# Block-causal attention and a three-way maxout FFN on one core: the limits of the weights' upper words on GpSimd, the weights' transfers begun by SyncE, other durations in the planner

## The chip, the cores and the metric

The kernel runs on one core of a Trainium2 chip. The metric is the device time in microseconds. The core has five engines, each with its own queue worked through in order: TensorE (PE; its weight loads are shown as PEld), VectorE (DVE), ScalarE (ACT), GpSimd (POOL) and SyncE (SP), which here only begins transfers. An instruction waits at the head of its queue until the semaphores that it needs are there, and all that stands behind it waits too.

## What is computed

```python
# q, k, v: (8 batches, 8 heads, 576, 64)
scores = scale * np.matmul(q, k.transpose(0, 1, 3, 2))
mask = block_i >= block_j                      # blocks of 64 rows
scores = np.where(mask, scores, -1000000000.0)
attn = np.exp(scores - max) / (sum + 1e-09)
x = (attn @ v).transpose(0, 2, 1, 3).reshape(4608, 512)
h = np.maximum(np.maximum(x @ w1, x @ w2), x @ w3)   # w1, w2, w3: 512 x 768
out = h @ w_out                                       # 768 x 512
```

The FFN's four weight matrices come as float64; the kernel reads each number as two 32-bit words.

## The kernel before

**Attention.** Heads are worked on in pairs, four pairs per batch. A pair loads q, k (`nat`) and v (`vn`), turns q and k (`kq`), multiplies them (`qk`, and `qk4` for the last 64 rows), takes the row limits (`top`, VectorE, L422), the exponential (ScalarE, L606, L960), the sum and its reciprocal (VectorE), scales (`scale`, on GpSimd or ScalarE, whichever the planner finds free), turns the probabilities and multiplies with v (`pv`, L1000). Batch 0 is done in two halves, front and back pairs, and turns on TensorE (`raise_qk`, `raise_p`, `raise4`) with copies by VectorE or ScalarE (`place...`, L251 or L249). From batch 1 on VectorE turns (`turn_qk` L917, `turn` L629), and SyncE moves the turned blocks (`move`, L641, `pt<-pz`).

**FFN.** A chunk is one half of a batch's rows (256 or 320 columns). For each of six blocks f of the hidden width it has three products with four parts each (`product`, L1118), each product as three matmuls, since x and the weights are each split into a high and a low part; then maximum (`most`, L1133), split (`high`, `low`), and the projection (`project`, L1184).

**Weight units.** The weights are prepared once, in 24 units: unit u = 0 to 17 makes the split blocks of w1, w2 and w3, unit 18 to 23 those of w_out. A unit loads 512 KB (`load`, L292, a transfer begun by GpSimd), then works on 128x512 blocks: `size` on ScalarE (L302, the absolute value of the upper words), five steps on VectorE, namely `clamp` (L308, the limits), `shift` (L315), `sign` (L321), `power` (L327) and `rest` (L338), then `high` on ScalarE, `whole` on TensorE (L345 to L347) and `lower` on ScalarE. The buffers of `a` and `b` are called wo or osb in the profile. No product with a block can start before its unit is done. All 24 units fall in the first 150 us.

**The order.** All work is cut into jobs with a cost per engine, a rank and the jobs they come after. `in_order` is a planner: it plays the jobs through with these costs (`LAG` for the way from one engine to another, `dve()`, `act()`, `pool()` and the constants at the top for durations) and writes down which engine begins which job next; where a job has two engines it takes the first that is free. The program then has exactly this order on each queue. So a changed constant changes the order, and the choice between GpSimd and ScalarE, or ScalarE and VectorE, without any change in the work.

Of the kernel before, what the change touches and what calls it, by code (L numbers as in the profile page):

```python
# [11 lines left out]
I32 = mybir.dt.int32  # L12
# [13 lines left out]

TO_PE = 250.0
LAG = {
    "PE": {"PE": 0.0, "ACT": 200.0, "DVE": 200.0, "POOL": 200.0, "SP": 200.0},
    "ACT": {"PE": TO_PE, "ACT": 0.0, "DVE": 90.0, "POOL": 160.0, "SP": 150.0},  # L30
    "DVE": {"PE": TO_PE, "ACT": 130.0, "DVE": 0.0, "POOL": 155.0, "SP": 150.0},
    "POOL": {"PE": TO_PE, "ACT": 130.0, "DVE": 130.0, "POOL": 0.0, "SP": 150.0},
    "SP": {"PE": 100.0, "ACT": 100.0, "DVE": 100.0, "POOL": 100.0, "SP": 0.0},
}
SEND = 620.0
LOAD = 540.0
ASK = 1000.0
# [3 lines left out]

GAP = 60.0
SMALL = 130.0

RAISE = 215.0
DEBUG = False
# [95 lines left out]
def dve(n, fast=False):  # L142
    return 100.0 + n / (1.92 if fast else 0.96)


def act(n, psum=True):
    return (105.0 if psum else 135.0) + n / 1.2


def pool(n):  # L150
    return 120.0 + 2.6 * n


@with_exitstack
def kernel(
# [11 lines left out]
    nc = tc.nc  # L167
# [17 lines left out]
    TURN = 12  # L185
# [71 lines left out]
    class Unit:  # L257


        def __init__(self, u, src, dst, n, prior, *early, first=None):  # L260
            self.src, self.dst, self.n, self.u = src, dst, n, u
            self.last = n == DO
            rank = DELAY + PACE * u


            self.tag = f"wo{dst}" if self.last else f"w{u}"
            self.temps = (f"wo{u % NF}",) if not self.last else (f"wo{4 + dst % 2}",) if dst < 4 else ("osb", "osb")
            j = self.issued = job(
                {"POOL": ASK},
                rank - 8,  # L270
                self.load,
                after=(prior and prior.issued, first, *(e.sized for e in early if e)),
                take=(self.tag,) if self.last else (),
            )
            j = job({}, 0, lambda eng: None, after=(j,), lasts=MOVE, moved=1600.0)
            j = self.sized = job({"ACT": act(512, False)}, rank, self.size, after=(j,), take=self.temps)
            for step, fast in (
                (self.clamp, True),
                (self.shift, True),
                (self.sign, False),  # L280
                (self.power, True),
                (self.rest, False),
            ):
                c = dve(512, fast)
                j = job({"DVE": c}, rank, step, after=(j,), take=("left",) if step == self.rest else (), lasts=c + GAP)
            j = job({"ACT": act(512, False)}, rank, self.high, after=(j,))
            j = job({"PE": 6 * pe(512)}, rank, self.whole, after=(j,), take=("pm",), give=(*self.temps, "left"))
            self.done = job({"ACT": act(512)}, rank, self.lower, after=(j,), give=("pm",))
# [144 lines left out]
    def norm_cost(n):  # L433
        return {"POOL": 160.0 + 1.86 * n, "ACT": 235.0 + n / 1.2}

# [6 lines left out]
    class Head:  # L442
# [7 lines left out]
        def plan(self, t0):  # L450

            pair, part, self.exps, self.inv = self.pair, self.pair.part, {}, {}
            for n, ts in enumerate(part.groups):
                apart, r = None, t0 + (SECOND if part.beside and ts == part.later else n)
                for t in ts:
                    m = P * (t + 1)
                    d = job(
                        {"DVE": dve(m) + 120.0},
                        r + 1,
# [6 lines left out]
                    if t != ts[-1]:  # L466
                        apart = job({}, 0, lambda eng: None, after=(d,), lasts=GAP)
                    self.exps[t] = job({"ACT": act(m) + 240.0}, r + 2, self.exp, t, after=(d,), take=(f"p{t}",))
                join([self.exps[t] for t in ts], BANK)
# [175 lines left out]
    class Pair:  # L645
# [106 lines left out]
        def plan4(self, first, tq, last):  # L752
            asked = job({"ACT": 2 * act(64, False)}, first - TURN + 2, self.ask, after=(tq,), take=("q8",))
            tops = []
            for a in range(2):
                last = job({"PE": 4 * pe(64 if a else 512)}, first + 3 + a, self.qk4, a, after=(asked, last), take=BANK)
                tops.append(
                    job(
                        {"DVE": dve(64 if a else 512) + 120.0},
                        first + 4 + a,  # L760
# [264 lines left out]
    left = {}  # L1025
# [197 lines left out]
    rank = 0  # L1223
# [54 lines left out]
```

## Time and profile before

| | before |
|---|---|
| median of 3 runs | 927.47 us (925.59 to 927.82) |
| profiled execution | 927.53 us |
| its span, first to last instruction | 925.7 us |
| TensorE busy | 895.4 us, 97% |
| VectorE busy | 530.1 us, 57% |
| ScalarE busy | 479.6 us, 52% |
| GpSimd busy | 246.3 us, 27% |
| mean granted TensorE clock | 0.994 |

The profile is of one execution. A share is an average over the span, so it is read beside the windows: the first 150 us, with the weight units and batch 0, look different from the rest. A busy time is the union of an engine's instructions; a wait of an instruction that has already started, for another engine's hold on something, is inside its duration and not in the idle time. Chain: the work that ended last, followed back to what released it.

### The profile page before, as it was taken

The page shows a single profiled execution, that of the slowest core. Times are in us where ns is not written, and L with a number is a line of the kernel's source. Part 1 is how long each engine was busy: PE and PEld are TensorE (multiplying, and loading weights), DVE is VectorE, ACT ScalarE, POOL GpSimd, SP SyncE. Part 2 cuts the span into 40 slices and gives each one's busy share as a digit, 9 for nine tenths or more (in the row PEclk, how much of TensorE's full clock was granted, in tenths as well). Part 3 has the DMA queues.
Part 4 walks back from the last instruction along what each step waited for, and adds up shares of the span by engine and source line. Part 5 has one row for each costly group of instructions (what it writes and reads, how often), then busy time and mean ns, then how long its engine had stood idle before and what let it go on. Part 6 is the DMA issues. An engine that isn't in the chain of part 4 may idle for free.

```text
span 925.7 us, 16909 instructions
## 1 busy us (share of the span) xinstructions
PE 895.4 (97%) x5880; PEld 744.7 (80%) x5880; DVE 530.1 (57%) x1555; ACT 479.6 (52%) x1359; POOL 246.3 (27%) x377
## 2 busy tenths in 40 slices
PE   6798899999999999999999999999999999999998
PEld 4456667886988888888888888888888888899997
DVE  4999688786674655465574655465664655431101
ACT  3777557655564555556464555555464654522111
POOL 3522232333231222223132222223131322222101
PEclk9999999999999999999999999999999999999999
DMA  6841535576644554555533555555543543330010
GB/s 197 232 144 54 125 85 126 127 141 145 131 94 100 113 123 105 133 110 124 118 86 80 114 123 107 123 111 132 110 99 75 115 113 84 95 73 24 1 35 23
DMA packets 226132, 98.36 MB, mean 106 GB/s; under 512 B 189696, under 2 KB 218368, under 8 KB 226048
## 3 DMA queue, kind: packets, MB, share of 16 engines
q1 hardware_dynamic: 208192, 82.35, 40.3%
q0 software_dynamic: 3456, 12.58, 4.0%
q10 hardware_dynamic: 14400, 2.36, 1.4%
q8 instruction: 46, 0.75, 0.3%
q14 instruction: 38, 0.31, 0.1%
HBM read 41.94 MB, written 9.44 MB: 56 GB/s over the span
## 4 chain that ended last, share of the span: by engine, by line
PE 90%; DVE 5%; ACT 1%; issue 1%; DMA 1%; POOL 1%; ACTq 0%; SPq 0%; DVEq 0%; POOLq 0%
PE pm L1118 49%; PE pm L1184 16%; PE sb L1000 10%; PE sb L933 9%; PE sb L940 3%; PE pm L345 1%; DVE sb L422 1%; DVE wo L321 1%; DVE wo L308 1%; DVE left L338 1%; POOL p L440 1%; DMA nat<-in_q_dram 1%; PE sb L558 0%; ACT w L249 0%; DVE wo L315 0%
## 5 line engine op out<-in xcount | busy, mean ns | idle before, releaser
L1118 PE MATMUL pm<-xh,w 128*128 128x320 f32 (+1 forms) x2304 | 500.2, 304 | 0.7 <-ACT w L249 0.7
L1118 PEld LDWEIGHTS pm<-xh,w 128*128 128x128 f32 x2304 | 379.9, 190 | 20.1 <-issue 15.3
L1118 PE MATMUL pm<-xl,w 128*128 128x256 f32 (+1 forms) x1152 | 341.2, 296 | 0.7 <-POOL xl L254 0.5
L1118 PEld LDWEIGHTS pm<-xl,w 128*128 128x128 f32 x1152 | 219.0, 190 | 7.2 <-issue 5.3
L422 DVE CUSTOM_DVE_ANT_0 sb<-sb,mask 128x512 f32<-128x512 f32 (+3 forms) x288 | 144.8, 529 | 138.3 <-PE sb L940 70.0
L1133 DVE TENSOR_TENSOR m<-pm,m 128x256 f32<-128x256 f32 (+1 forms) x192 | 87.3, 455 | 167.1 <-PE pm L1118 159.0
L606 ACT ACTIVATE p<-sb,nm 128x128 f32<-128x128 f32 (+3 forms) x256 | 134.2, 528 | 75.0 <-DVE nm L422 62.8
L254 POOL TENSOR_TENSOR hl<-m,hh 128x256 fp32r<-128x256 f32 x96 | 71.6, 746 | 316.9 <-ACT hh L249 285.1
L629 DVE STREAM_TRANSPOSE pz<-p 128x512 f32<-128x512 f32 (+1 forms) x280 | 136.4, 525 | 21.8 <-ACT p L438 20.0
L440 POOL TENSOR_TENSOR p<-p,rs 128x384 f32<-128x384 f32 (+4 forms) x129 | 90.0, 719 | 186.7 <-DVE rs L750 180.8
L1184 PE MATMUL pm<-wo,hh 128*128 128x512 f32 x384 | 119.2, 391 | 0.0
L249 ACT CAST hh<-m 128x256 fp32r<-128x256 f32 x96 | 39.0, 406 | 121.3 <-DVE m L1133 120.7
L438 ACT ACTIVATE p<-p,rs 128x512 f32<-128x512 f32 (+4 forms) x159 | 89.6, 608 | 20.2 <-DVE rs L750 12.9
L1000 PE MATMUL sb<-pt,vn 128*64 128x320 f32 (+4 forms) x840 | 90.4, 362 | 4.0 <-ACT p L606 2.5
L254 POOL TENSOR_TENSOR xl<-x,xh 128x256 fp32r<-128x256 f32 (+1 forms) x64 | 51.9, 815 | 156.1 <-ACT xh L249 150.0
L933 PE MATMUL sb<-kq 64*128 64x256 f32 (+3 forms) x512 | 88.5, 466 | 2.6 <-DVE kq L251 2.0
L1000 PEld LDWEIGHTS sb<-pt,vn 128*64 128x64 f32 x840 | 55.3, 137 | 37.4 <-issue 5.0
L1184 PEld LDWEIGHTS pm<-wo,hh 128*128 128x128 f32 x384 | 71.0, 188 | 15.1 <-issue 0.3
L933 PEld LDWEIGHTS sb<-kq 64*128 64x128 f32 x512 | 45.5, 192 | 38.1 <-issue 21.7
L1184 PE MATMUL pm<-wo,hl 128*128 128x512 f32 x192 | 74.8, 390 | 0.0
L249 ACT COPY m<-pm 128x256 f32<-128x256 f32 (+1 forms) x96 | 38.3, 399 | 45.9 <-PE pm L1118 33.3
L249 ACT COPY osb<-pm 128x512 f32<-128x512 f32 x36 | 21.1, 587 | 75.7 <-PE pm L1184 75.7
(82 smaller groups left out, 762.5 us busy)
## 6 DMA issues: line engine op xcount, KB each, us to landing
pt<-pz SPq DMA_DIRECT2D x224, 200.0 KB, 3.9
w<-in_moe_w_dram POOLq DMA_DIRECT2D x18, 512.0 KB, 5.6
vn<-in_v_dram SPq DMA_DIRECT2D x64, 128.0 KB, 2.4
out_dram<-osb SPq DMA_DIRECT2D x32, 256.0 KB, 2.1
nat<-in_k_dram SPq DMA_DIRECT2D x112, 72.0 KB, 2.3
nat<-in_q_dram SPq DMA_DIRECT2D x96, 72.0 KB, 2.7
wo<-in_moe_w_out_dram POOLq DMA_DIRECT2D x6, 512.0 KB, 4.2
nat<-in_q_dram ACTq DMA_DIRECT2D x16, 72.0 KB, 3.2
```

What stands on the lines that cost most here:

```text
L249: nc.scalar.copy(dst, src)
L254: {"DVE": nc.vector, "POOL": nc.gpsimd}[eng].tensor_tensor(out=dst, in0=a, in1=b, op=ALU.subtract)
L422: nc.vector.tensor_tensor_reduce(out=ps, in0=ps, in1=hidden, scale=-SCALE, scalar=first, op0=ALU.add, op1=ALU.min, accum_out=out_)
L438: nc.scalar.mul(p, p, r)
L440: nc.gpsimd.tensor_tensor(out=p, in0=p, in1=r.broadcast_to([P, p.shape[1]]), op=ALU.mult)
L606: nc.scalar.activation(dst, src, AF.Exp, bias=nm[:, c : c + 1], scale=-1.0, accum_out=sm[:, c : c + 1])
L629: nc.vector.transpose(dst, p[:, 0 : n * P])
L933: nc.tensor.matmul(ps, self.q[h.own, P * t : P * (t + 1)], self.k[h.own, 0:w], start=True, stop=True)
L1000: nc.tensor.matmul(o[h.own].rearrange("p (i u) -> p i u", u=n)[:, :, c0 : c0 + z - a], self.vn[:, kt, h.j, :], h.pt[:, :, h.off + a : h.of ...
L1118: nc.tensor.matmul(self.ps, w[i, f][:, c, :], xx, start=(c == 0 and s == 0), stop=(c == NC - 1 and s == 2))
L1133: nc.vector.tensor_tensor(out=m, in0=ps, in1=m, op=ALU.max)
L1184: nc.tensor.matmul(self.po[: self.rows], h, w[f], start=(f == 0 and s == 0), stop=(f == NF - 1 and s == 2))
```

## The change

Three things change. `clamp` is issued to GpSimd instead of VectorE. The 24 transfers of weights are begun by SyncE instead of GpSimd, between its other loads. And the planner's constants are others, so the order on all five queues is another. What is computed, its shapes and its buffers stay the same. Line numbers behind L280 are three higher after the change.

```diff
-TO_PE = 250.0
+TO_PE = 180.0
 LAG = {
     "PE": {"PE": 0.0, "ACT": 200.0, "DVE": 200.0, "POOL": 200.0, "SP": 200.0},
-    "ACT": {"PE": TO_PE, "ACT": 0.0, "DVE": 90.0, "POOL": 160.0, "SP": 150.0},
-    "DVE": {"PE": TO_PE, "ACT": 130.0, "DVE": 0.0, "POOL": 155.0, "SP": 150.0},
...
+    "ACT": {"PE": TO_PE, "ACT": 0.0, "DVE": 140.0, "POOL": 180.0, "SP": 150.0},
+    "DVE": {"PE": TO_PE, "ACT": 120.0, "DVE": 0.0, "POOL": 240.0, "SP": 150.0},
...
 def dve(n, fast=False):
-    return 100.0 + n / (1.92 if fast else 0.96)
+    return 68.0 + n / (1.92 if fast else 0.96)
...
@@ class Unit
             j = self.issued = job(
-                {"POOL": ASK},
+                {"SP": LOAD},
                 rank - 8,
                 self.load,
...
-                c = dve(512, fast)
-                j = job({"DVE": c}, rank, step, after=(j,), take=("left",) if step == self.rest else (), lasts=c + GAP)
+                c = dve(512, fast) + (130.0 if fast else 80.0)
+                e = "DVE"
+                if step == self.clamp:
+                    e, c = "POOL", pool(512)
+                j = job({e: c}, rank, step, after=(j,), take=("left",) if step == self.rest else (), lasts=c + GAP)
...
         def load(self, eng):
...
-            nc.gpsimd.dma_start(st.rearrange("p (c f) -> p c f", f=2 * self.n), self.src.bitcast(I32))
+            nc.sync.dma_start(st.rearrange("p (c f) -> p c f", f=2 * self.n), self.src.bitcast(I32))
...
         def clamp(self, eng):
-            nc.vector.tensor_scalar(
+            nc.gpsimd.tensor_scalar(
                 out=self.a, in0=self.a, scalar1=LOW, scalar2=TOP, op0=ALU.max, op1=ALU.min
             )
...
     def norm_cost(n):
-        return {"POOL": 160.0 + 1.86 * n, "ACT": 235.0 + n / 1.2}
+        return {"POOL": 250.0 + 1.5 * n, "ACT": 190.0 + n / 1.2}
```

The other constants (`GAP`, `SMALL`, `RAISE`, `act()`, `pool()`, the sums added to `top`, `exp` and `ask`) change in the same way. Three places show what this does to the queues. A name such as wo_842 is one buffer of a unit.

First, VectorE's queue where units 12 to 14 are prepared, before the change (L308 is `clamp`, L315 `shift`, L321 `sign`, L327 `power`, L338 `rest`):

```order
L308 TENSOR_SCALAR wo_842<-wo_842 128x512
L327 TENSOR_SCALAR wo_781<-wo_781 128x512
L315 TENSOR_SCALAR wo_842<-wo_842 128x512
L321 SCALAR_TENSOR_TENSOR wo_842<-w_684,wo_842 128x512
L327 TENSOR_SCALAR wo_842<-wo_842 128x512
L308 TENSOR_SCALAR wo_881<-wo_881 128x512
L338 SCALAR_TENSOR_TENSOR left<-w_432,wo_700 128x512
L315 TENSOR_SCALAR wo_881<-wo_881 128x512
```

and after it, about the same units (L318 is `shift`, L324 `sign`, L330 `power`, L341 `rest`, L425 `top`):

```order
L318 TENSOR_SCALAR wo_839<-wo_839 128x512
L1136 TENSOR_TENSOR m<-pm,m 128x256
L324 SCALAR_TENSOR_TENSOR wo_839<-w_633,wo_839 128x512
L318 TENSOR_SCALAR wo_868<-wo_868 128x512
L330 TENSOR_SCALAR wo_839<-wo_839 128x512
L425 ISA sb,nm<-sb,mask 128x512
L425 ISA nm 128x1
L341 SCALAR_TENSOR_TENSOR left<-w_612,wo_717 128x512
L324 SCALAR_TENSOR_TENSOR wo_868<-w_664,wo_868 128x512
```

The row of `clamp` is gone, and steps of attention stand between the unit's steps. On GpSimd's queue the units' rows were transfers (L292):

```order
L254 TENSOR_TENSOR xl_619<-x_0_592,xh_601 128x256
L992 COPY p_578<-p_578 128x64
L292 DMA w_684<-in_moe_w_dram 128x4x256
L292 DMA w_706<-in_moe_w_dram 128x4x256
L292 DMA w_722<-in_moe_w_dram 128x4x256
L254 TENSOR_TENSOR xl_787<-x_1_761,xh_773 128x320
```

and are now limits (L311):

```order
L254 TENSOR_TENSOR xl_546<-x_0_537,xh_539 128x256
L311 TENSOR_SCALAR wo_584<-wo_584 128x512
L311 TENSOR_SCALAR wo_592<-wo_592 128x512
L311 TENSOR_SCALAR wo_600<-wo_600 128x512
L311 TENSOR_SCALAR wo_626<-wo_626 128x512
L311 TENSOR_SCALAR wo_659<-wo_659 128x512
L311 TENSOR_SCALAR wo_671<-wo_671 128x512
L254 TENSOR_TENSOR xl_699<-x_1_681,xh_687 128x320
```

Six limits stand in a row there, those of units 5 to 10. Second, VectorE's queue ahead of the first `turn_qk` of batch 1 (the long transpose), before:

```order
L251 COPY kq<-sb 128x2x64
L338 SCALAR_TENSOR_TENSOR left<-w_722,wo_890 128x512
L251 COPY pz<-sb 128x4x4x32
L251 COPY pz<-sb 128x3x4x32
L917 STREAM_TRANSPOSE kq<-nat 128x1152
```

and after:

```order
L251 COPY kq<-sb 128x2x64
L324 SCALAR_TENSOR_TENSOR wo_946<-w_853,wo_946 128x512
L324 SCALAR_TENSOR_TENSOR wo_995<-w_880,wo_995 128x512
L251 COPY pz<-sb 128x4x4x32
L251 COPY pz<-sb 128x3x4x32
...
L341 SCALAR_TENSOR_TENSOR left<-w_727,wo_933 128x512
L251 COPY pz<-sb 128x4x4x32
L251 COPY pz<-sb 128x3x4x32
L251 COPY pz<-sb 128x4x16
L920 STREAM_TRANSPOSE kq<-nat 128x1152
```

Thirteen rows stand between the copy and the transpose instead of three. Third, SyncE's queue, where it loads `nat` (k) and `vn` (v) of the back pairs of batch 0, before:

```order
L902 DMA vn_76<-in_v_dram 128x4x64 x2
L907 DMA vn_76<-in_v_dram 64x2x64
L875 DMA nat<-in_k_dram 128x4x64 x2
L881 DMA nat<-in_k_dram 64x2x64
L902 DMA vn_75<-in_v_dram 128x4x64 x2
L907 DMA vn_75<-in_v_dram 64x2x64
```

and after (L295 is the transfer of a weight unit, here units 9 to 15):

```order
L905 DMA vn_76<-in_v_dram 128x4x64 x2
L910 DMA vn_76<-in_v_dram 64x2x64
L295 DMA w_595<-in_moe_w_dram 128x4x256
L295 DMA w_602<-in_moe_w_dram 128x4x256
L295 DMA w_612<-in_moe_w_dram 128x4x256
L295 DMA w_633<-in_moe_w_dram 128x4x256
L295 DMA w_664<-in_moe_w_dram 128x4x256
L905 DMA vn_75<-in_v_dram 128x4x64 x2
L910 DMA vn_75<-in_v_dram 64x2x64
L295 DMA w_694<-in_moe_w_dram 128x4x256
L295 DMA w_727<-in_moe_w_dram 128x4x256
```

Seven transfers of weights stand between the loads of v, and the load of k is further back.

## Rows read from the trace of the kernel before

**Rows 1.** The page: busy time by engine; VectorE's busy tenths in 40 slices.

```profile
PE 895.4 (97%) x5880; PEld 744.7 (80%) x5880; DVE 530.1 (57%) x1555; ACT 479.6 (52%) x1359; POOL 246.3 (27%) x377
...
DVE  4999688786674655465574655465664655431101
```

**Rows 2.** Windows of 25 us: length, then PE, PEld, DVE, ACT, POOL busy, PEclk, DMA.

```profile
0.00:25.00 25.00, 16.04 (x70) 10.52 (x70) 12.32 (x48) 10.56 (x32) 9.92 (x23) 1.00 0.73 200
25.00:50.00 25.00, 18.47 (x92) 11.02 (x93) 23.44 (x65) 19.63 (x55) 9.93 (x14) 0.93 0.75 225
50.00:75.00 25.00, 23.02 (x130) 15.88 (x126) 24.07 (x59) 19.00 (x48) 10.54 (x13) 0.93 0.43 127
75.00:100.00 25.00, 22.67 (x129) 15.21 (x130) 20.42 (x50) 17.50 (x42) 7.67 (x11) 1.00 0.23 63
100.00:125.00 25.00, 22.24 (x136) 15.72 (x135) 19.43 (x44) 15.12 (x39) 5.14 (x6) 1.00 0.43 94
125.00:150.00 25.00, 22.96 (x136) 16.81 (x135) 19.57 (x55) 15.39 (x42) 9.11 (x14) 0.93 0.33 79
...
250.00:275.00 25.00, 25.00 (x172) 20.81 (x171) 16.71 (x49) 14.28 (x43) 7.78 (x14) 1.00 0.51 104
```

**Rows 3.** The chain that ended last, in order of time: start, us, what.

```profile
73.92 1.30 DVE wo L308
...
137.56 2.21 PE sb L1000 x20
```

**Rows 4.** The same chain, near 212 us.

```profile
212.23 3.69 DMA pt<-pz
```

**Rows 5.** VectorE's instructions by line and form, 13 to 150 us: busy, mean ns, idle before.

```profile
L338 DVE SCALAR_TENSOR_TENSOR left<-w,wo 128x512 fp32r<-128x512 uint32 x18 | 13.4, 744 | 1.7 <-PE pm L347 1.7
L321 DVE SCALAR_TENSOR_TENSOR wo<-w,wo 128x512 int32<-128x512 int32 x18 | 12.6, 698 | 0.1
L308 DVE TENSOR_SCALAR wo<-wo 128x512 f32<-128x512 f32 x22 | 11.7, 542 | 0.8 <-ACT wo L302 0.8
L327 DVE TENSOR_SCALAR wo<-wo 128x512 int32<-128x512 int32 x22 | 11.4, 516 | 0.2
L315 DVE TENSOR_SCALAR wo<-wo 128x512 int32<-128x512 int32 x22 | 11.1, 510 | 0.2
...
L321 DVE SCALAR_TENSOR_TENSOR wo<-wo,wo 128x512 int32<-128x512 int32 x4 | 4.0, 1003 | 0.1
```

**Rows 6.** Timeline, VectorE at 60 and 73 us, GpSimd at 73 us: start, us, instruction.

```profile
60.42 0.42 DVE L308 TENSOR_SCALAR wo<-wo 128x512 f32<-128x512 f32 x1
...
61.34 0.69 DVE L321 SCALAR_TENSOR_TENSOR wo<-w,wo 128x512 int32<-128x512 int32 x1
...
73.84 1.37 DVE L308 TENSOR_SCALAR wo<-wo 128x512 f32<-128x512 f32 x1
...
73.76 1.16 POOL L440 TENSOR_TENSOR p<-p,rs 128x576 f32<-128x576 f32 x1 [1.19 <-DVE rs L977]
```

**Rows 7.** GpSimd's instructions by line and form, 13 to 150 us.

```profile
L254 POOL TENSOR_TENSOR xl<-x,xh 128x320 fp32r<-128x320 f32 x4 | 3.5, 868 | 25.3 <-ACT xh L249 25.3
...
L440 POOL TENSOR_TENSOR p<-p,rs 128x512 f32<-128x512 f32 x3 | 3.3, 1096 | 0.0
```

**Rows 8.** Window 13 to 150 us: all engines as in rows 2; GpSimd's L292 alone.

```profile
13.00:150.00 137.00, 118.96 (x657) 80.65 (x657) 116.40 (x298) 93.10 (x242) 48.22 (x64) 0.96 0.46 126
...
13.00:150.00 137.00, 15.94 (x22) 0.96 0.46 126
```

**Rows 9.** VectorE's plain copies of turned probabilities, one form, 13 to 150 us.

```profile
L251 DVE COPY pz<-sb 128x256 f32<-128x256 f32 x6 | 2.5, 414 | 0.1
```

**Rows 10.** Waits: VectorE's longest from 13 to 150 us, SyncE's longest of the span.

```profile
DVE kq L917 <- DMA nat<-in_k_dram: 3.8, 1, 3.8
...
SPq L902 <- PE sb L1000: 235.2, 32, 24.1
```

**Rows 11.** The page, transfers: count, KB each, median us from issue to landing.

```profile
w<-in_moe_w_dram POOLq DMA_DIRECT2D x18, 512.0 KB, 5.6
```

More of the change, by code (lines that the diff above doesn't have):

```diff
@@ L24 @@
 EPS = 1e-9
-TO_PE = 250.0
+TO_PE = 180.0
 LAG = {
     "PE": {"PE": 0.0, "ACT": 200.0, "DVE": 200.0, "POOL": 200.0, "SP": 200.0},
-    "ACT": {"PE": TO_PE, "ACT": 0.0, "DVE": 90.0, "POOL": 160.0, "SP": 150.0},
-    "DVE": {"PE": TO_PE, "ACT": 130.0, "DVE": 0.0, "POOL": 155.0, "SP": 150.0},
-    "POOL": {"PE": TO_PE, "ACT": 130.0, "DVE": 130.0, "POOL": 0.0, "SP": 150.0},
+    "ACT": {"PE": TO_PE, "ACT": 0.0, "DVE": 140.0, "POOL": 180.0, "SP": 150.0},
+    "DVE": {"PE": TO_PE, "ACT": 120.0, "DVE": 0.0, "POOL": 240.0, "SP": 150.0},
+    "POOL": {"PE": TO_PE, "ACT": 90.0, "DVE": 130.0, "POOL": 0.0, "SP": 150.0},
     "SP": {"PE": 100.0, "ACT": 100.0, "DVE": 100.0, "POOL": 100.0, "SP": 0.0},
@@ L40 @@
 TURNED = 4400.0
-GAP = 60.0
-SMALL = 130.0
-RAISE = 215.0
+GAP = 85.0
+SMALL = 100.0
+RAISE = 110.0
 DEBUG = False
@@ L142, in dve @@
 def dve(n, fast=False):
-    return 100.0 + n / (1.92 if fast else 0.96)
+    return 68.0 + n / (1.92 if fast else 0.96)
 def act(n, psum=True):
-    return (105.0 if psum else 135.0) + n / 1.2
+    return (52.0 if psum else 88.0) + n / 1.2
 def pool(n):
-    return 120.0 + 2.6 * n
+    return 150.0 + 2.15 * n
 @with_exitstack
@@ L275, in __init__ @@
             j = job({}, 0, lambda eng: None, after=(j,), lasts=MOVE, moved=1600.0)
-            j = self.sized = job({"ACT": act(512, False)}, rank, self.size, after=(j,), take=self.temps)
+            j = self.sized = job({"ACT": act(512, False) + 65.0}, rank, self.size, after=(j,), take=self.temps)
             for step, fast in (
@@ L457, in plan @@
                     d = job(
-                        {"DVE": dve(m) + 120.0},
+                        {"DVE": dve(m) + 35.0},
                         r + 1,
@@ L467, in plan @@
                         apart = job({}, 0, lambda eng: None, after=(d,), lasts=GAP)
-                    self.exps[t] = job({"ACT": act(m) + 240.0}, r + 2, self.exp, t, after=(d,), take=(f"p{t}",))
+                    self.exps[t] = job({"ACT": act(m) + 200.0}, r + 2, self.exp, t, after=(d,), take=(f"p{t}",))
                 join([self.exps[t] for t in ts], BANK)
@@ L752, in plan4 @@
         def plan4(self, first, tq, last):
-            asked = job({"ACT": 2 * act(64, False)}, first - TURN + 2, self.ask, after=(tq,), take=("q8",))
+            asked = job({"ACT": 510.0}, first - TURN + 2, self.ask, after=(tq,), take=("q8",))
             tops = []
@@ L758, in plan4 @@
                     job(
-                        {"DVE": dve(64 if a else 512) + 120.0},
+                        {"DVE": dve(64 if a else 512) + 65.0},
                         first + 4 + a,
@@ L766, in plan4 @@
                 )
-            e = job({"ACT": act(512) + act(64) + 480.0}, first + 5, self.exp4, after=tops, take=("p4",), give=2 * BANK)
+            e = job({"ACT": act(512) + act(64) + 350.0}, first + 5, self.exp4, after=tops, take=("p4",), give=2 * BANK)
             inv = job({"DVE": SMALL}, first + 6, self.sum4, after=(e,), lasts=SMALL + GAP)
```

## The prediction, made before the changed kernel was run

> **What bounds the kernel now.** I read the busy shares and the forty slices first, then the windows of 25 us, then the chain of waits, then the costs of single instructions in the stretch that the windows point to. Over the whole span TensorE is busy 97% and VectorE 57% [rows 1], which says that TensorE bounds the kernel. The windows say when that holds. From about 150 us on TensorE has no idle time at all, 25.00 of 25 us as in the window 250 to 275. Before, it is idle for 8.96, 6.53, 1.98, 2.33, 2.76 and 2.04 us in the first six windows, 24.6 us together, and it starts only 70 to 136 matmuls in each, against 172 later [rows 2]. In the same windows VectorE is busy 23.4 and 24.1 and then 19.4 to 20.4 of 25 us. So there are two programs in this trace: up to about 140 us VectorE feeds TensorE too slowly, and after that nothing but the amount of matmul work counts. The chain agrees: at 73.92 us it runs through weight preparation on VectorE, and from 137.56 us it stays on TensorE [rows 3]. One exception follows: near 212 us the chain leaves TensorE once more for a transfer of the turned probabilities [rows 4].
>
> It follows that time can be won only ahead of 140 us, that a microsecond less of VectorE's queue there brings later matmuls forward by about as much, and that the 24.6 us of idle time (of which the first 4.8 us are the first loads) bound the sum.
>
> **The limits leave VectorE.** Each of 24 weight units has five VectorE steps, and the first, `clamp`, goes to GpSimd. In the stretch from 13 to 150 us 22 of these instructions are busy for 11.7 us, 542 ns each [rows 5]; two more, on other buffers, at the undisturbed 0.42 us [rows 6] make it 12.5 us. VectorE is the engine whose queue binds, so all of it counts: **-12.5 us**. On GpSimd the same instruction is not in the trace. Its nearest rows there are the product over 128x512 at 1.10 us and the difference over 128x320 at 0.87 us [rows 7]; I take 1.1, bounds 0.87 and 1.3 (a fifth more). 24 x 1.1 = 26.4 us. GpSimd is busy 48.2 of the 137 us, 15.9 of them beginning the weights' transfers [rows 8]. Those go, so it ends at 48.2 - 15.9 + 26.4 = 58.7 us, and its own queue doesn't bind. A unit's chain gets about 0.7 us longer. In the new order `shift` waits for GpSimd, and VectorE's queue stands behind it; the new order puts copies, tops and steps of other units between, as the order shows, so I price this wait at nothing. Were that cover gone, it would cost up to 24 x 0.7 = 17 us.
>
> **What the two engines do to each other.** An undisturbed step over 512 columns takes 0.42 us; one that started at 73.84 us took 1.37 while GpSimd had a product in hand from 73.76 to 74.92 [rows 6]. So a VectorE step waits until GpSimd's instruction ends. Over the undisturbed 0.42 and 0.69 us, the other four steps lose (0.510 - 0.42) x 22 = 2.0, (0.516 - 0.42) x 22 = 2.1, (0.698 - 0.69) x 18 + (1.003 - 0.69) x 4 = 1.4 and (0.744 - 0.69) x 18 = 1.0 us, 6.5 together [rows 5, 6]. These 96 steps stay, and GpSimd computes more. If only its arithmetic holds VectorE up, that grows from 48.2 - 15.9 = 32.3 to 58.7 us, a factor of 1.8, and 6.5 becomes 11.8 us: +5.3. If beginning transfers holds it up as much, the factor is 58.7 / 48.2 = 1.2, and the cost is +1.4. The long wait that I can see was arithmetic, so I take **+5.3 us**, with 1.4 as the other end.
>
> The Trainium skill, "SBUF — State Buffer", section "Who interferes with whom", says that a VectorE instruction in a two-port mode and a GpSimd instruction exclude each other for the whole of the one that came first, and that writing the descriptors of a GpSimd-issued transfer needs the same ports. The 1.37 us agree with its first half. Its second half would count the transfers' beginnings too, and by it the sum would be 3.9 us better than mine; its first half speaks against putting more work on GpSimd beside VectorE, and that is the first rival below.
>
> **Copies.** In the order VectorE has 51 plain copies where it had 47: 11 more of turned probabilities, seven fewer of others. At 0.41 us [rows 9] four are **+1.6 us**. ScalarE, which gets these seven and loses the eleven, is busy 93.1 of 137 us [rows 8] and doesn't bind.
>
> **The new order.** VectorE's longest wait in the stretch is 3.8 us, for the keys of the first pair of batch 1, ahead of `turn_qk` [rows 10]. The order puts three rows between the copy whose matmuls free the loads' buffer and this transpose now, some 1.9 us of work (0.69, 0.68 and 0.55), and 13 rows after the change, about 6.6 us. That would cover the wait. But in SyncE's queue the loads of two weight units now stand right ahead of that load. I take half: **-1.9 us**, bounds 0 and -3.8. The remaining moves of the order (attention of batch 0 earlier against the weights, matmuls of the first chunk ahead of the units they don't need) put more work ahead of TensorE while weights are made; I count nothing for them. After 220 us TensorE is never idle, its order differs by less than 1.4 us of matmuls at any place that I compared, and the same work remains: 0.
>
> **The transfers go to SyncE.** 24 issues, 15.9 us on GpSimd for 22 of them, land in SyncE's queue. That queue mostly waits: its `vn` loads wait 235 us in all for matmuls that free their buffer [rows 10]. That is also the danger, since SyncE works in order: units 9 to 13 stand behind a `vn` load that needs the values matmul of the last front pair, 14 and 15 behind a later one. From that values matmul to unit 9's own TensorE had 104 matmuls before and has 153 in the new order, some 28 us at the 130 and 136 per 25 us of [rows 2]. A weight block lands 5.6 us after its issue [rows 11], five in a row take up to four issues more, and the seven steps of a unit add up to 4.6 us at the durations above. So it is hidden: 0. If the cover is gone, a unit is late by about the 5.6 us of one transfer, once.
>
> **The stall at 212 us.** It hangs on turns that VectorE does and matmuls that TensorE does in the same stretch; both come forward alike, so it stays: 0. Were it to go, it would be worth up to the 3.7 us of that transfer [rows 4].
>
> **The sum.** -12.5 + 5.3 + 1.6 - 1.9 = -7.5 us. The profiled execution took 927.53 us (span 925.7 and 1.8 around it), the median of the runs is 927.47, so they may be taken as one: 927.5 - 7.5 = **920.0 us**. With the kind ends of the unknowns it is -12.5 + 1.4 + 1.6 - 3.8 - 3.7 = -17, or 910.5; with the unkind ones, ahead of any rival, -12.5 + 6.3 + 1.6 = -4.6 (clamps of 1.3 us, a factor of 63.5 / 32.3), or 923.
>
> **Rivals.** *First, the exclusion eats the gain, and more.* The clamp of one unit ends and GpSimd begins the next instruction just as VectorE is told to go on with `shift`; the new GpSimd order has six clamps in a row. If every clamp holds up one VectorE step by 0.8 us (1.37 - 0.42 was 0.95), that is 24 x 0.8 = 19.2 instead of 5.3 us, and the sum is -12.5 + 19.2 + 1.6 - 1.9 = +6.4: **934 us**. It turns into a loss once the 96 steps wait more than 6.5 + 12.8 = 19.3 us in all, 0.2 us each where they wait 0.07 now. For it speaks the one visible long wait, against it that most steps of before have no wait at all. *Second, VectorE is freed and nothing comes of it*: the chain of a unit (ScalarE, GpSimd, VectorE, ScalarE, TensorE) is longer by 0.7 us and a crossing, weights arrive at the pace of before, and TensorE, in order, waits for them: 925 to 929. For it: weights stand later against the other work in the new order, by some 5 us of matmuls. Against: they stood early before, and TensorE has that work to do meanwhile. *Third, late weights through SyncE's queue*: -7.5 + 5.6 = -1.9, or 925.6. *Fourth, better than forecast*: transfers' beginnings held VectorE up as much as arithmetic, and the wait and the stall go: 910 to 914.
>
> TensorE's granted clock is 0.93 in three of the early windows, 25 to 75 and 125 to 150 us [rows 2], each after idle time; 7% of 25 us is 1.7 us where TensorE binds, nothing where it waits. I leave it in the range.
>
> **How the numbers follow.** Forecast, 914 to 924: 0.50. Better, 909 to 914: 0.12. VectorE freed for nothing: 0.18. Late weights: 0.07, half of it still faster. Exclusion: 0.13, nearly all slower. A measurement of this kernel tells about 0.3%, 2.8 us, from no change. So faster 0.66, same 0.20, slower 0.14. The range goes from 909 to 931: below it lie few of the better cases, above it half of the first rival.
>
> **What would show it.** VectorE's busy time from 13 to 150 us falls from 116.4 to about 109; GpSimd shows 24 clamps near 1.1 us; `shift` and `power` rise from 0.51 to about 0.6 us, and to 0.8 if the first rival holds; the first window with 25.00 us of TensorE ends some 8 us earlier; no wait of ScalarE's `size` for a weight transfer. I am wrong if VectorE's busy time doesn't fall, if TensorE's idle time before 150 us stays near 24 us although it does, or if idle time of TensorE appears after 220 us.

## The result and the profile after

| | before | after |
|---|---|---|
| median | 926.53 us (925.26 to 927.82, 4 runs) | 917.73 us (916.16 to 919.61, 4 runs) |
| profiled execution, span | 927.53 us, 925.7 us | 916.16 us, 914.0 us |

The ratio is 0.9906, with a 95% interval of 0.9881 to 0.9931: 8.8 us faster. Below, a difference is always between a kernel's median and that of the kernel before, measured on the same chip in the same comparison.

The page of after, answering [rows 1] (busy by engine; VectorE in 40 slices):

```profile
PE 892.6 (98%) x5880; PEld 742.3 (81%) x5880; DVE 529.6 (58%) x1535; ACT 468.9 (51%) x1353; POOL 285.9 (31%) x379
...
DVE  4889986986545756564555756564654755421111
```

The windows of after, columns as in [rows 2], and the stretch of [rows 8]:

```profile
0.00:25.00 25.00, 15.50 (x71) 10.50 (x72) 12.97 (x50) 9.99 (x32) 9.64 (x21) 1.00 0.71 191
25.00:50.00 25.00, 20.73 (x106) 13.68 (x105) 20.20 (x52) 20.31 (x57) 14.77 (x13) 0.86 0.53 140
50.00:75.00 25.00, 24.54 (x147) 17.38 (x147) 23.67 (x54) 20.11 (x48) 22.91 (x14) 1.00 0.71 221
75.00:100.00 25.00, 23.92 (x141) 16.62 (x139) 24.66 (x55) 17.11 (x41) 15.61 (x12) 1.00 0.35 79
100.00:125.00 25.00, 23.73 (x147) 16.98 (x144) 21.29 (x46) 16.60 (x40) 14.77 (x11) 1.00 0.55 123
125.00:150.00 25.00, 24.90 (x140) 18.26 (x139) 21.12 (x65) 16.19 (x48) 8.27 (x8) 1.00 0.52 109
...
13.00:150.00 137.00, 127.22 (x717) 88.91 (x716) 120.60 (x305) 96.69 (x251) 83.47 (x66) 0.98 0.55 143
```

TensorE's idle time in these six windows is 9.50 + 4.27 + 0.46 + 1.08 + 1.27 + 0.10 = 16.7 us, where it was 24.6 [rows 2]: 7.9 of the 8.8 us. The place is the forecast one. But VectorE's busy time from 13 to 150 us did not fall: it was 116.40 [rows 8] and is 120.60. That window is fixed in time and holds more work after the change, since work comes earlier; a comparison up to the same instruction follows with e5.

The limits in after, GpSimd's groups by form from 13 to 150 us:

```profile
L311 POOL TENSOR_SCALAR wo<-wo 128x512 f32<-128x512 f32 x22 | 45.8, 2094 | 16.8 <-ACT wo L305 16.8
...
L311 POOL TENSOR_SCALAR osb<-osb 128x512 f32<-128x512 f32 x2 | 3.8, 1917 | 6.0 <-ACT osb L305 6.0
```

One takes 1.92 us when nothing disturbs it and 2.09 in the mean; the forecast had 1.1. The four steps left on VectorE, answering [rows 5] (same view; L318 is `shift`, L324 `sign`, L341 `rest`, L330 `power`):

```profile
L318 DVE TENSOR_SCALAR wo<-wo 128x512 int32<-128x512 int32 x22 | 14.6, 672 | 3.6 <-POOL wo L311 3.6
L324 DVE SCALAR_TENSOR_TENSOR wo<-w,wo 128x512 int32<-128x512 int32 x18 | 14.3, 796 | 0.1
L341 DVE SCALAR_TENSOR_TENSOR left<-w,wo 128x512 fp32r<-128x512 uint32 x18 | 14.1, 782 | 2.1 <-PE pm L350 2.1
...
L330 DVE TENSOR_SCALAR wo<-wo 128x512 int32<-128x512 int32 x22 | 12.5, 572 | 0.1
```

All four got longer, and `shift` now stands idle for limits, 3.6 us in all.

What TensorE did from 25 to 100 us, by line (PE alone, columns as in rows 5). Before, where L1118 is a product of the FFN and L345 the first part of `whole`, two matmuls per weight unit:

```profile
L345 PE MATMUL pm<-wo,plus 128*128 128x512 f32 x30 | 17.5, 669 | 0.7 <-ACT w L249 0.7
L1118 PE MATMUL pm<-xh,w 128*128 128x256 f32 x70 | 17.3, 309 | 0.7 <-ACT w L249 0.7
...
L1118 PE MATMUL pm<-xl,w 128*128 128x256 f32 x35 | 9.8, 281 | 0.0
```

and after (L1121 is the product, L348 that part of `whole`):

```profile
L1121 PE MATMUL pm<-xh,w 128*128 128x256 f32 x86 | 21.0, 306 | 0.0
L348 PE MATMUL pm<-wo,plus 128*128 128x512 f32 x30 | 16.0, 615 | 0.0
L1121 PE MATMUL pm<-xl,w 128*128 128x256 f32 x43 | 12.3, 285 | 0.0
```

By 100 us weights are no further: 30 matmuls, 15 units, in both (the last unit's first matmul starts at 145.10 us instead of 148.34). But 86 + 43 = 129 matmuls of products are done in that stretch instead of 105. That speaks for the order rather than for a relieved VectorE, and the experiments test it.

### The profile page after: what moved, and what is told of

Read it like the earlier page. It is cut to its first block, busy times and chain, and to the rows that moved or that the text cites. A ratio compares the mean times of both kernels' runs of the same rounds, so it can differ in the third digit from the quotient of the medians.

```text
span 914.0 us, 16879 instructions
## 1 busy us (share of the span) xinstructions
PE 892.6 (98%) x5880; PEld 742.3 (81%) x5880; DVE 529.6 (58%) x1535; ACT 468.9 (51%) x1353; POOL 285.9 (31%) x379
## 4 chain that ended last, share of the span: by engine, by line
PE 88%; DVE 6%; ACT 2%; POOL 2%; DMA 1%; issue 1%; ACTq 0%; SPq 0%; DVEq 0%; POOLq 0%
PE pm L1121 49%; PE pm L1187 16%; PE sb L1003 9%; PE sb L936 9%; PE sb L943 3%; DVE wo L324 1%; POOL wo L311 1%; DVE sb L425 1%; DVE left L341 1%; PE pm L348 1%; DVE wo L330 1%; DVE wo L318 1%; ACT wo L305 1%; DVE pz L251 0%; POOL p L443 0%
## 5 line engine op out<-in xcount | busy, mean ns | idle before, releaser
L1121 PE MATMUL pm<-xh,w 128*128 128x320 f32 (+1 forms) x2304 | 499.8, 304 | 0.5 <-ACT xh L249 0.5
L1121 PEld LDWEIGHTS pm<-xh,w 128*128 128x128 f32 x2304 | 379.4, 190 | 19.7 <-issue 15.1
L1121 PE MATMUL pm<-xl,w 128*128 128x256 f32 (+1 forms) x1152 | 340.8, 296 | 0.5 <-POOL xl L254 0.5
L1121 PEld LDWEIGHTS pm<-xl,w 128*128 128x128 f32 x1152 | 218.6, 190 | 6.9 <-issue 5.3
L425 DVE CUSTOM_DVE_ANT_0 sb<-sb,mask 128x512 f32<-128x512 f32 (+3 forms) x288 | 143.2, 529 | 132.1 <-PE sb L943 75.5
L443 POOL TENSOR_TENSOR p<-p,rs 128x384 f32<-128x384 f32 (+4 forms) x131 | 96.9, 757 | 252.0 <-DVE rs L753 205.9
L609 ACT ACTIVATE p<-sb,nm 128x512 f32<-128x512 f32 (+3 forms) x256 | 133.6, 527 | 80.9 <-DVE nm L425 75.4
L441 ACT ACTIVATE p<-p,rs 128x128 f32<-128x128 f32 (+4 forms) x157 | 89.0, 597 | 19.0 <-DVE rs L753 12.8
```

The costliest lines, as they stand in the source:

```text
L425: nc.vector.tensor_tensor_reduce(out=ps, in0=ps, in1=hidden, scale=-SCALE, scalar=first, op0=ALU.add, op1=ALU.min, accum_out=out_)
L441: nc.scalar.mul(p, p, r)
L443: nc.gpsimd.tensor_tensor(out=p, in0=p, in1=r.broadcast_to([P, p.shape[1]]), op=ALU.mult)
L609: nc.scalar.activation(dst, src, AF.Exp, bias=nm[:, c : c + 1], scale=-1.0, accum_out=sm[:, c : c + 1])
L1121: nc.tensor.matmul(self.ps, w[i, f][:, c, :], xx, start=(c == 0 and s == 0), stop=(c == NC - 1 and s == 2))
```

## The experiments

The planner's constants set an order, and the line that issues an instruction sets its engine. So the engines can be switched back at that line alone while every queue of TensorE, ScalarE and the rest keeps its order. That gives a table of two orders by two engines for the limits by two for the transfers. The theory was the prediction's: VectorE is relieved. The rival: the gain is the order, and the two moves add little or cost.

| order | limits on | transfers by | median | to before | ratio, 95% interval |
|---|---|---|---|---|---|
| before | GpSimd | GpSimd (e5) | 943.22 | +17.3 | 1.0187, 1.0166 to 1.0208 |
| before | VectorE | SyncE (e6) | 923.36 | -2.5 | 0.9966, 0.9952 to 0.9980 |
| before | GpSimd | SyncE (e4) | 938.26 | +11.9 | 1.0124, 1.0104 to 1.0144 |
| after | VectorE | GpSimd (e1) | 914.92 | -11.4 | 0.9872, 0.9853 to 0.9891 |
| after | VectorE | SyncE (e2) | 912.88 | -13.5 | 0.9857, 0.9837 to 0.9876 |
| after | GpSimd | GpSimd (e3) | 926.15 | -0.2 | 0.9997, 0.9985 to 1.0009 |
| after | GpSimd | SyncE (after) | 917.73 | -8.8 | 0.9906, 0.9881 to 0.9931 |

**e1 and e2: the new order with the limits back on VectorE.** The edits to after (the second one in e1 alone):

```diff
         def clamp(self, eng):
-            nc.gpsimd.tensor_scalar(
+            nc.vector.tensor_scalar(
...
-            nc.sync.dma_start(st.rearrange("p (c f) -> p c f", f=2 * self.n), self.src.bitcast(I32))
+            nc.gpsimd.dma_start(st.rearrange("p (c f) -> p c f", f=2 * self.n), self.src.bitcast(I32))
```

> The changed kernel's order on every queue, but the limits are issued by VectorE and the transfers begun by GpSimd, at the same places of the order. My theory (VectorE's queue before 150 us decides, and the limits' leaving it is most of the gain): 24 x 0.42 us come back to VectorE and some 6 us of mutual waits go, so about 922 to 924 us where before takes 926.5 and the change 917.7. Rival A (the order made with the new durations is the gain, the engines don't matter): 916 to 919. Rival B (the transfers on SyncE are the gain): 925 or more.

> The change without its first part: the limits are issued by VectorE at the same places of the new order, transfers stay with SyncE. My theory: 921 to 924, close to the order alone. Rival A (order): 916 to 919, as the change. Rival B (transfers on SyncE): 916 to 920 as well, but then the order alone is slower than this by 4 us or more.

Measured: 914.92 and 912.88 us. The order alone, with both engines as before, gives 11.4 us. e2 is faster than either kernel. VectorE's groups of e2, 13 to 150 us:

```profile
L318 DVE TENSOR_SCALAR wo<-wo 128x512 int32<-128x512 int32 x22 | 12.5, 578 | 0.0
...
L311 DVE TENSOR_SCALAR wo<-wo 128x512 f32<-128x512 f32 x22 | 9.1, 414 | 0.8 <-ACT wo L305 0.8
```

The limits cost VectorE 9.1 us there, and nothing waits for them. The theory falls: to take them away from VectorE makes this order 4.7 us slower (13.5 against 8.8).

**e3: the new order, limits on GpSimd, transfers begun by GpSimd** (of the edits above, the second alone).

> The change without its second part: transfers are begun by GpSimd at the same places of the new order, limits stay on GpSimd. A limit takes 1.9 us there, so GpSimd's queue carries 24 issues of 0.6 to 0.8 us more, about 100 of 137 us. My theory (transfers cost nothing on SyncE and little on GpSimd): 917 to 921. Rival B (transfers on SyncE are the gain): 923 or more.

Measured: 926.15 us, no different from before. With limits and transfers in one queue the whole gain of the order is gone; the limits cost 11.2 us here (e1 to e3). GpSimd's timeline in e3 shows the queue (start, us, instruction; L295 is the beginning of a transfer):

```profile
53.37 1.92 POOL L311 TENSOR_SCALAR wo<-wo 128x512 f32<-128x512 f32 x1 [1.40 <-ACT wo L305]
55.24 1.57 POOL L295 DMA_DIRECT2D w<-in_moe_w_dram  x2
56.84 4.04 POOL L311 TENSOR_SCALAR wo<-wo 128x512 f32<-128x512 f32 x2
60.83 0.81 POOL L295 DMA_DIRECT2D w<-in_moe_w_dram  x1
61.68 1.94 POOL L311 TENSOR_SCALAR wo<-wo 128x512 f32<-128x512 f32 x1
```

**e4, e5 and e6: the old order with both moves, the limits alone, the transfers alone.** To the kernel before:

```diff
-            nc.gpsimd.dma_start(st.rearrange("p (c f) -> p c f", f=2 * self.n), self.src.bitcast(I32))
+            nc.sync.dma_start(st.rearrange("p (c f) -> p c f", f=2 * self.n), self.src.bitcast(I32))
...
-            nc.vector.tensor_scalar(
+            nc.gpsimd.tensor_scalar(
                 out=self.a, in0=self.a, scalar1=LOW, scalar2=TOP, op0=ALU.max, op1=ALU.min
```

> The old order on every queue, with the limits on GpSimd and the transfers begun by SyncE. My theory: VectorE loses 12.5 us and gets some 6 back in waits, but a unit's chain is 1.5 us longer where the old order puts shift close behind the limits, so VectorE's queue stands: 921 to 925. Rival A (order): 926 or more. Rival B (transfers): 918 to 922.

> The kernel before in its own order on every queue; only the limits are issued to GpSimd, the transfers stay there too. The prediction's step (VectorE's queue binds, 12.5 us leave it, a unit's chain is 0.7 us longer) gives 916 to 922. The rival that the runs so far favour, a limit of 1.9 us on GpSimd in each unit's chain against 0.4 on VectorE, priced 11.2 us under the new order with the transfers on GpSimd, gives 936 to 947, above the 938.3 of limits and transfers both moved, since the beginnings of transfers and the limits then stand in one queue. Within 3 us of 926 would say that the loss in the earlier run of the old order came from the transfers.

> The kernel before in its own order; only the 24 weight transfers are begun by SyncE. If beginning a transfer on GpSimd costs VectorE or GpSimd's own attention work something in any order, it gains the 2.0 us measured under the new order with the limits on VectorE: 923 to 925. If it is free, 926. If SyncE's queue holds weights back in the order of before, which has less attention work ahead of TensorE, it is later by one transfer or more: 930 to 938, and then the 938.3 of both moved is partly this.

Measured: 938.26, 943.22 and 923.36 us. So the limits' move, the part of the change that was to pay most, costs 17.3 us by itself. Why, e5 shows. VectorE's waits from 13 to 150 us in e5 (waiting line, what for: us in all, times, longest; L315 is `shift`, L308 the limits):

```profile
DVE wo L315 <- POOL wo L308: 15.6, 8, 3.2
...
DVE osb L315 <- POOL osb L308: 1.7, 1, 1.7
```

The chain of waits of e5, cut to 75 to 100 us, where it goes from unit to unit (start, us, what):

```profile
79.79 0.22 POOL p L992
80.01 1.93 POOL wo L308
...
86.12 2.17 POOL wo L308
88.29 0.02 issue
88.32 0.04 DVE wo L315
```

VectorE waits at the head of its queue while GpSimd first finishes attention work (L992) and then takes 1.9 us for the limits. e5 has the order of before on every queue, so VectorE's time up to the same instruction can be compared. I take the sum over the last 64 rows of batch 1's first pair (L971, L974 in the order of after). VectorE's own timeline has it at

```profile
147.05 0.15 DVE L971 SCALAR_TENSOR_TENSOR rs<-sm 128x1 f32<-128x1 f32 x1
```

before, and in e5 at

```profile
160.98 0.15 DVE L971 SCALAR_TENSOR_TENSOR rs<-sm 128x1 f32<-128x1 f32 x1
```

The windows up to there, columns as in [rows 2], before:

```profile
0.00:147.05 147.05, 122.45 (x671) 83.42 (x673) 116.31 (x304) 94.75 (x249) 49.37 (x72) 0.97 0.49 134
```

and e5:

```profile
0.00:160.98 160.98, 129.95 (x680) 89.20 (x681) 111.79 (x280) 95.72 (x249) 96.15 (x96) 0.94 0.45 122
```

With 24 instructions fewer VectorE is busy 4.5 us less (116.31 to 111.79) and idle 18.5 us more (30.74 to 49.19). `shift` waits 19.1 us for limits up to there (15.6 for wo, 3.5 for osb, of which the second wait lies behind 150 us). So waiting for the limits accounts for all of the added idle time. The same pair in the new order, after and e2 (136.48 and 133.01 us at that instruction), after first:

```profile
0.00:136.48 136.48, 119.90 (x676) 83.44 (x677) 112.45 (x285) 92.49 (x243) 81.88 (x75) 0.97 0.54 144
```

and e2:

```profile
0.00:133.01 133.01, 117.61 (x674) 81.34 (x675) 114.77 (x308) 91.88 (x243) 35.59 (x52) 1.00 0.55 148
```

Here the limits' leaving takes 2.3 us off VectorE's busy time (114.77 to 112.45) and adds 5.8 us of idle time (18.24 to 24.03), 4.1 of it waits of `shift` for limits. In both orders more waiting is added than queue time comes free. What the order does, before against e2 shows, both with the limits on VectorE (e2 has the transfers on SyncE too): the instruction comes 14.0 us earlier, 1.5 of it less busy time and 12.5 less idle time. From before to after it comes 10.6 us earlier, 3.9 of it less busy time and 6.7 less idle time.

e6 shows that beginning transfers on SyncE is a small gain of its own, 2.5 us; from e1 to e2 it is 2.0, where the single runs overlap. With the limits on GpSimd it is worth more: 5.4 us from e5 to e4 and 8.6 from e3 to after, by their differences to before.

**e7 and e8: planned anew.** All the new durations; limits told and issued on VectorE; transfers on GpSimd (e7) or SyncE (e8). The edit to after that both have, with the issue on VectorE as in e2:

```diff
                 c = dve(512, fast) + (130.0 if fast else 80.0)
-                e = "DVE"
-                if step == self.clamp:
-                    e, c = "POOL", pool(512)
-                j = job({e: c}, rank, step, ...
+                j = job({"DVE": c}, rank, step, ...
```

> The planner of after with all its new durations, but limits planned and issued on VectorE, transfers planned and issued on GpSimd, as before: the order is planned anew. If the gain is that the planner knows the durations better, it comes within 3 us of the 914.9 measured for the order of after with these engines: 912 to 918. If the gain is a property of the one order that was planned round limits on GpSimd (units spread over more attention work because a limit is told as 1.25 us), it goes back to 922 to 928.

> The planner of after with all its new durations, limits planned and issued on VectorE, transfers planned and issued on SyncE. If knowing the durations is what counts, a plan that also knows where the limits run is at least as good as the 912.9 measured for the order of after with limits put on VectorE: 909 to 914. If the order planned for slow limits is the better one for its own reasons, 916 to 924.

Measured: 913.37 (ratio 0.9862, 0.9841 to 0.9883) and 913.05 us (0.9871, 0.9843 to 0.9899; its six runs go from 911.95 to 917.46). So the gain isn't tied to the one order that was made round limits on GpSimd.

**e9 and e10: which durations?** To before, in e9 one line; to e7, in e10 the reverse, and with it the length told for `size` on ScalarE:

```diff
-                c = dve(512, fast)
+                c = dve(512, fast) + (98.0 if fast else 48.0)
```

```diff
-            j = self.sized = job({"ACT": act(512, False) + 65.0}, ...
+            j = self.sized = job({"ACT": act(512, False) + 12.0}, ...
...
-                c = dve(512, fast) + (130.0 if fast else 80.0)
+                c = dve(512, fast) + 32.0
```

> The kernel before, its engines and all its constants but one: a unit's five steps on VectorE are told 98 and 48 ns longer, 465 and 681 instead of 367 and 633 (measured: 510 to 542 and 698 to 744). The order is planned anew. If the gain of the new order is that the planner no longer takes VectorE to be free while it still prepares weights, this one figure brings most of the 12.5 us: 913 to 918. If it comes from the other durations and ways (attention, copies, the step to TensorE), 922 to 928.

> The other half: engines as before, all new durations, but the unit's steps told 367 and 633 as before. If the unit's steps are the cause, 922 to 928. If the rest is, 913 to 918. Something between in both halves would say that the order's gain can't be put down to one figure.

Measured: 912.86 (0.9855, 0.9834 to 0.9876) and 916.54 us (0.9895, 0.9879 to 0.9912). One line that makes the planner believe in longer unit steps brings 13.6 us; the other durations without it bring 9.9. (e10 is not exactly the other half: its `size` is told 527 ns, where before has 562 and e7 580.) Each by itself brings most of the gain, so the gain can't be put down to one figure. The window of e9 from 13 to 150 us:

```profile
13.00:150.00 137.00, 127.39 (x725) 87.83 (x725) 123.88 (x328) 101.39 (x272) 53.81 (x68) 1.00 0.55 146
```

With no instruction moved to another engine by hand, VectorE is idle 13.1 us of the 137, where it was 20.6 [rows 8], and TensorE is busy 127.39 instead of 118.96.

**e11 and e12: the limit's price.** Two edits to after, one in each:

```diff
-                    e, c = "POOL", pool(512)
+                    e, c = "POOL", 2000.0
```

```diff
-                out=self.a, in0=self.a, scalar1=LOW, scalar2=TOP, op0=ALU.max, op1=ALU.min
+                out=self.a, in0=self.a, scalar1=TOP, scalar2=None, op0=ALU.min
```

> The kernel after, engines as there, limits on GpSimd; the planner is told 2.00 us for a limit there instead of 1.25 (measured 2.09), and makes the order anew. If the price of the limits on GpSimd (4.8 us against the same order with them on VectorE) is only an order made for too short a duration, 911 to 914. If it is the longer chain of a unit itself, which no order takes away, 916 to 922.

> The kernel after in its own order, but the limit on GpSimd is one operation with the upper bound alone, instead of two; the lower bound is left out. If the 1.92 us of the instruction are two passes of arithmetic, it takes 1.0 to 1.2 us, about the 1.1 that the prediction took, and the kernel gets 3 to 5 us of the 4.8 back: 913 to 915. If it is one pass at a fixed pace, 1.9 us stay, and the time stays at 917 to 918. If the prediction's own price of 1.1 had been the whole of its error on GpSimd, 913 or below is what it says.

Measured: 913.72 (0.9864, 0.9844 to 0.9884) and 917.49 us (0.9903, 0.9885 to 0.9921). In e11 the limits still take 2.08 us each on GpSimd, as its groups show, and `shift` hardly waits for them. GpSimd's group by form, 13 to 150 us:

```profile
L311 POOL TENSOR_SCALAR wo<-wo 128x512 f32<-128x512 f32 x22 | 45.5, 2081 | 14.9 <-ACT wo L305 14.9
```

VectorE's wait for it, as in e5:

```profile
DVE wo L318 <- POOL wo L311: 1.2, 2, 0.7
```

That wait was 15.6 us in e5 (limits cost 17.3), 3.6 in after (4.7) and is 1.2 in e11, which is level with e8 (12.8 us faster than before, both). So with an order made for its real length a slow limit on GpSimd costs nothing that these runs can tell, and gains nothing either. That is one order of each kind, and the orders of e7 to e10 differ by up to 3.7 us among themselves. e12's groups on GpSimd:

```profile
L311 POOL TENSOR_SCALAR wo<-wo 128x512 f32<-128x512 f32 x22 | 36.0, 1647 | 21.2 <-ACT wo L305 21.2
L311 POOL TENSOR_SCALAR osb<-osb 128x512 f32<-128x512 f32 x2 | 3.0, 1488 | 6.1 <-ACT osb L305 6.1
```

One operation instead of two takes 1.49 us undisturbed, neither of the two values expected, and the 0.45 us saved per limit move the time by nothing that can be measured (after: 917.73). `shift` waits only 0.9 us for limits in e12, so that wait isn't what the limits cost in the new order, or not alone. There is a second one. TensorE's waits for GpSimd's scaling of the probabilities (L443), 13 to 150 us, in after:

```profile
PE sb L561 <- POOL p L443: 3.2, 2, 2.5
...
PE sb L989 <- POOL p L443: 1.3, 1, 1.3
```

and in e2:

```profile
PE sb L561 <- POOL p L443: 0.7, 1, 0.7
```

The timelines of GpSimd and TensorE in after show the longest of them:

```profile
25.30 3.80 POOL L311 TENSOR_SCALAR wo<-wo 128x512 f32<-128x512 f32 x2 [2.15 <-ACT wo L305]
29.07 0.61 POOL L443 TENSOR_TENSOR p<-p,rs 128x256 f32<-128x256 f32 x1
...
29.74 1.33 PE L561 MATMUL sb<-plus,p 128*128 128x128 f32 x5 [2.50 <-POOL p L443]
```

Two limits stand ahead of the scaling in GpSimd's queue, and TensorE waits 2.50 us for it; in e2, without them, this scaling begins at 27.01 us. These waits are 4.5 us in after, 1.8 in e12 and 0.7 in e11. As e12 is no faster than after, the runs don't settle how the 4.7 us divide.

## Why the prediction was right, and where it was wrong

Faster was right, and 917.7 us lies 2.3 us under the forecast of 920.0. But the reason was wrong, and that the sum came so near is luck: the limits and what they do to the other engine were put at -12.5 + 5.3 = -7.2 us and cost 4.7, the order with its copies was put at -0.3 and gives 11.4.

**The limits leave VectorE, -12.5 us, and the wait for them, "at nothing": the first step that failed.** The move costs 17.3 us alone, 4.7 us in the change as made. Two things eat the 12.5 us. The steps that stay get longer (below), so that up to the same instruction VectorE is busy only 4.5 us less in e5, 2.3 less from e2 to after. And `shift` waits for the limits. This was priced "at nothing", since copies and tops stand between; in the new order that holds for most units (3.6 us of waiting), in the old one it doesn't (15.6). "Were that cover gone" had 17 us as its price, from a unit's chain made 0.7 us longer. The loss of e5 is of that size, but the chain grew by 1.98 (a limit on GpSimd in e5) less 0.54 [rows 5], 1.4 us a unit, there, so the agreement is partly chance. The ground given, "VectorE is the engine whose queue binds, so all of it counts", left out the 20.6 of 137 us in which VectorE already stood idle [rows 8]; whether that alone would have kept the relief from counting isn't shown, since no run takes the limits off VectorE without putting them elsewhere.

**The price of a limit on GpSimd, 1.1 us, bounds 0.87 and 1.3.** Measured 1.92 undisturbed, 2.09 in the mean. The nearest rows were tensor-tensor instructions of the same size [rows 7], and those were no bound for one with two scalars. GpSimd's busy time from 13 to 150 us became 83.5, not 58.7 us, and "its own queue doesn't bind" failed with it: TensorE waits 4.5 us for scaling on GpSimd, 0.7 in the same order with the limits on VectorE (e2; before had 2.0).

**The two engines' mutual waits, +5.3 us.** By the same formula: (0.672 - 0.42) x 22 = 5.5, (0.572 - 0.42) x 22 = 3.3, (0.796 - 0.69) x 18 = 1.9 and (0.782 - 0.69) x 18 = 1.7, with 0.5 for four `sign` on other buffers at 0.818: 12.9 in all, 6.4 more than before. The size was about right, the picture wasn't. VectorE's timeline of after, while GpSimd does limits without a pause:

```profile
52.19 0.82 DVE L318 TENSOR_SCALAR wo<-wo 128x512 int32<-128x512 int32 x1 [0.96 <-POOL wo L311]
53.05 0.69 DVE L324 SCALAR_TENSOR_TENSOR wo<-w,wo 128x512 int32<-128x512 int32 x1
54.08 0.82 DVE L318 TENSOR_SCALAR wo<-wo 128x512 int32<-128x512 int32 x1 [0.34 <-POOL wo L311]
54.82 0.41 DVE L330 TENSOR_SCALAR wo<-wo 128x512 int32<-128x512 int32 x1
55.16 0.68 DVE L324 SCALAR_TENSOR_TENSOR wo<-w,wo 128x512 int32<-128x512 int32 x1
```

and GpSimd's:

```profile
50.24 12.32 POOL L311 TENSOR_SCALAR wo<-wo 128x512 f32<-128x512 f32 x6 [2.15 <-ACT wo L305]
```

A step that begins as a limit begins takes 0.82 instead of 0.42 us; the next ones run undisturbed, at 0.69, 0.41 and 0.68, within the same 2 us of a limit. So in these rows a limit holds VectorE up for some 0.4 us, not until it ends, and rival 1 (24 steps at 0.8 us, 934 us) did not come.

The Trainium skill, "SBUF — State Buffer", section "Who interferes with whom", says that of a VectorE instruction in a two-port mode, which a `tensor_scalar` can enter, and a GpSimd instruction the one that came first gets the shared ports for its whole instruction. The product of [rows 6] agreed with that, 1.37 us; for a limit these rows do not: `power` at 54.82 us, a `tensor_scalar`, took 0.41 us while limits followed each other without a pause. Of a transfer begun by GpSimd that stalls on VectorE the section says that the stall disappears with HWDGE, the way that SyncE's transfers take. That agrees with the 2.0 to 8.6 us above, though these runs can't tell ports from the place in the queue.

**"The remaining moves of the order ... I count nothing for them": the second step that failed, and the larger.** They are worth 11.4 us with the engines as before (e1), 13.5 with the transfers on SyncE (e2). The wait ahead of `turn_qk`, of which half was counted, is gone whole (3.8 us [rows 10]; no such wait in after), and other idle time of VectorE with it: 12.5 us less, before to e2, up to the instruction compared above. What the order changed can be read: 24 more matmuls of products stand between the units of 25 to 100 us. The prediction named this move itself ("put more work ahead of TensorE while weights are made") and then gave it no price. An upper bound was within reach: TensorE's 24.6 us of idle time less the first 4.8, 19.8 us, was what work at hand could fill.

**Transfers to SyncE, 0 us, as hidden.** The cover held: ScalarE's `size` waits 0.7 us in all for a weight transfer, so rival 3 did not come. But the gain on the side that they leave was missed: 2.0 us, and 8.6 with limits in that queue. **Copies, +1.6 us**, were not tested by themselves.

**The stall at 212 us stays, 0 us.** Right; the chain of after, 200 to 213 us, against [rows 4]:

```profile
200.41 3.60 DMA pt<-pz
```

**Rivals.** Rival 2 (VectorE freed for nothing, 925 to 929) comes nearest to what the limits' move does: a unit's chain gets longer and nothing comes of the relief. It was under-priced (17.3 us in e5) and hidden behind the order's gain, and it had TensorE wait for weights, where VectorE waited for the limits and TensorE for scaling. e3, 926.15, has its time, with transfers on GpSimd. Rival 4 (910 to 914) did not come; e2, 912.88, lies there, for another reason.

**The signs named.** VectorE's busy time didn't fall to 109 (120.60 in the fixed window; up to the same instruction it fell by 3.9 us), the limits weren't 1.1 us: both refuted, though the time came. `shift` and `power` at 0.67 and 0.57 for 0.6, and TensorE's idle time at 16.7 us, came. A prediction whose first sign fails is right by its sum alone.

**The sum, from runs:** order -11.4, transfers -2.0, limits +4.7, together -8.7 us; 8.8 were measured. They are steps from run to run, so they must add up. Taken in another sequence the parts differ (order -11.4, limits +11.2, transfers -8.6), since limits and transfers share a queue.

**What stays open.** Why the order of before is the slow one. Five orders made with other figures (after's, e7 to e10) give 912.9 to 916.5 us with the limits on VectorE; that each half of the durations brings most of the gain says as much about a poor draw before as about durations told rightly. Nor is the clock's part exact. TensorE's granted clock is 0.93 in three early windows of before [rows 2] and 1.00 from 13 to 150 us in e9. Before's own executions took 925.5 us at a mean clock of 0.998 and 927.5 at 0.994 (medians of 8 and 17), so by an estimate from these two the clock makes up some 2 to 3 of e9's 13.6 us. In after it is 0.86 from 25 to 50 us, where TensorE waited the 2.50 us above, and e2 has 1.00 in its 0 to 133.01 us: how much of their 4.7 us that is, when TensorE is idle 4.27 us of that window anyway, wasn't separated. One execution of e12, which has after's order, had a mean clock of 1.000 and took 916.24 us, 3.4 more than e2; that speaks against the clock as most of it.

## What to carry to other kernels

An engine that is nearly always busy is not yet the bound: look at its idle time in the same stretch too (12.5 of the 14.0 us that the order won up to the instruction compared were VectorE's idle time), and when work is moved away from it, price the waits for that work on the relieved engine and in the queue that the work joins. Where a planner sets the order, a change of its figures and a change of engines are two changes: freeze the order and switch the engines, and price them apart. An operation that moves to another engine needs a measured duration of that very form before the plan is made, since here the order made with 1.25 us told for 2.09 came out 4 us slower than the one made with 2.0.

## What the hardware showed that was not expected

- GpSimd takes 1.92 us for a limit with two scalar operations over 128x512 and 1.49 with one; VectorE takes 0.41 for the two. GpSimd's product of two tensors of that size took 1.10 [rows 7]. So the form with fewer tensors is the slower one there. The Trainium skill, "GPSIMD Engine Reference", section "3.1 Elementwise — side-by-side cycle accounting", has GpSimd about twice as slow as VectorE, measured on a sum of two tensors; here the ratio is 4.6.
- In the rows above a VectorE step that starts together with such a limit is held up for about 0.4 us of the limit's 1.92 (0.82 instead of 0.42), while one behind a product was held to its end (1.37 us [rows 6]).
- Beginning a 512 KB transfer keeps GpSimd for about 0.8 us (the L295 rows of e3), and 24 of them between limits of 1.9 us cost the kernel 8.6 us (e3 against after).
